# A second set of folded weights in the memory of the second block's first input, and folds split in two halves between other products

## The chip, the cores and the metric

The program runs on one core of a Trainium2 chip. The metric is device time in microseconds (us) of one execution; lower is better. The kernel before took 842.19 us as the median of three runs (839.94 to 844.63).

The engines are named as in the profile: PE is the matrix engine, PEld its weight loads, DVE the vector engine, ACT the scalar engine, POOL the GpSimd engine, SP the queue that issues the transfers. PE writes its products into eight accumulator banks (128 partitions by 512 floats each); ACT and DVE read them from there.

## The reference

The inputs are double-precision for the weights and single-precision in the kernel's arithmetic. What is computed, cut to what matters:

```python
def _attn_ref(q, k, v, phi):                 # 4 samples, 8 heads, 576 rows, head size 64, 32 memory slots
    a = softmax(phi, axis=2)
    k_m, v_m = einsum('bhsm,bhsd->bhmd', a, k), einsum('bhsm,bhsd->bhmd', a, v)
    attn = softmax(q @ k_m.T / sqrt(64))     # 576 x 32 for each sample and head
    return attn @ v_m

x = attention output, heads side by side     # 2304 x 512
y = ((x @ w_a) * (x @ w_b)) @ w_out          # first block, 1536 hidden features
h = y @ w_in                                 # second block, 2048 hidden features
out = (h * sigmoid(1.702 * h)) @ w_out2      # 2304 x 512
```

## The kernel before

**Folded weights.** The attention output is never formed. Since x is attn times v_m, the kernel multiplies the small v_m of a sample into the weights first ("fold") and then the attention into the result ("gated"). A folded weight belongs to one sample and one group of hidden features.

**Tiles and stages.** The first block goes through its 1536 hidden features in 6 groups g of 256 (w_a and w_b side by side, so 512 columns). In each group there are four samples b, each in two halves u of 288 rows. Samples 0 and 1 are called half A of a group here (pb = 0 in the code), samples 2 and 3 half B (pb = 1). Three kinds of products stand on PE, each in sets of 4 products:

- **fold** (line 637, matmuls on line 648): v_m of two samples (tile vhl) times one of the four row blocks r of the weights (tile wab_hl). 4 products, one for each r, of 3 matmuls with 512 columns. Each product fills one bank and has four readers: for each of the two samples ACT copies its half of the partitions to the high part of eff (line 663) and DVE subtracts to get the low part (line 665).
- **gated** (line 671, matmuls on line 687): the folded weights eff times attn. 4 products (j = 0, 1; w_a and w_b) of 6 matmuls with 288 columns. ACT copies the w_a product to gr (line 699), DVE multiplies the w_b product into it (line 702), ACT rounds the result to g1 (line 257), and POOL or DVE subtracts the rest (line 251).
- **proj** (line 708, matmuls on line 719): g1 times w_out. 4 products of 6 matmuls with 288 columns; DVE adds each to acc (line 736).

Every operand is split in a high and a low part, and each product is made in three passes. The folded weights of the samples of a half are in two tiles, eff (even sample) and eff_b (odd sample). Both halves of a group use these two tiles, so a fold can only be written when the gated products of the half before have been read.

**Weights.** Each group has 6 pieces of weights (4 of wab, 2 of w_out). A piece arrives as raw 64-bit words in one of three raw tiles and is decoded to single precision in one of four dm tiles: ACT (line 339), DVE or POOL (line 341), and then DVE three times (lines 345, 349, 354). From dm it is split into wab_hl or whl, by ACT (line 257) and POOL or DVE (line 251). There are four wab_hl tiles, one set; a tile is released by the fold of half B, which is the last to read it.

**What sets the order.** The program is written out in order by a planner (class Order). It keeps an estimated clock for each engine and lets one stream of work after another issue its next operation; a stream with a smaller priority number wins where two could start at about the same time. The planner also chooses the bank for each product (the one that it believes free first) and, where two engines can do a step, the engine. What it writes down is fixed: on the chip each engine runs its instructions in that order and waits for what they need. main() is the stream that gives the order of the products on PE: for each half, both gated sets of the first sample, the proj set left over from the half before (late), a gated set, a proj set, a gated set, then the fold for the half after, then two proj sets.

The tiles yhl[0, HI] and yhl[0, LO] (called y0_0 and y0_1) hold the first half of the second block's input, 4 x 1152 numbers for each partition. They are written only in the last group (split_y), and lie unused until then.

Of the kernel before, what the change touches and what calls it, by code (L numbers as in the profile page):

```python
# [15 lines left out]
HI, LO = 0, 1  # L16
# [130 lines left out]
def tile_mem_attention_moe_moe2(  # L147
# [16 lines left out]
    B, H, S, D = q.shape  # L164
# [13 lines left out]
    NHG = H // HG  # L178
# [4 lines left out]
    CW = G1 * P  # L183
    NG1 = F1 // CW
# [34 lines left out]
    eff_t = [p1.tile([P, NHG, 2, 2 * CW], F32R, name="eff")]  # L219
# [366 lines left out]
    def close_attention():  # L586

        for n in range(NU):
            for e in range(2):
                yield "mark", "attn", n, e  # L590
        for c in range(NHG):
            yield "mark", "eff", 0, B - 1, c, 0
        for s in list(bank_a.free):
            bank_m.free.append(s)
        pa.release()
        od.handicap[DVE] = W1
        nonlocal py, pz
        py = tc.alloc_tile_pool(name="py", bufs=1, side="right", reuse_waits="tile")
        for i in (HI, LO):
            yhl[0, i] = py.tile([P, KD, HT], F32R, name=f"y0_{i}")  # L600
        whl_s.free += slots(py, 1, [P, 2 * KD * G2 * P], "whl_b", F32R).free
        pz = tc.alloc_tile_pool(name="pz", bufs=1, side="right", reuse_waits="tile")
        wab_s.free += slots(pz, 2 * NHG, [P, 2 * 2 * CW], "wab_hl", F32R).free
        eff_t.append(pz.tile([P, NHG, 2, 2 * CW], F32R, name="eff_b"))
        vhl.extend(pz.tile([P, 2, 2 * NHG, P], F32R, name=f"vhl{i}") for i in range(B // 2))
        od.spawn(8, split_memory())


    py, pz, vhl, yhl, g1_t = None, None, [], {}, {}

    def fold0(b):
        for c in range(NHG):
# [21 lines left out]
                t1 = yield from hi_lo(t, dst[:, HI], dst[:, LO], src, 2 * D)  # L634
                od.mark(t1, "vhl", b, e)

    def fold(g, pb):
        t0 = 0.0
        for b in (2 * pb, 2 * pb + 1):
            for e in range(2):  # L640
                t0 = max(t0, (yield "mark", "vhl", b, e))
        outs = []
        for r in range(2 * NHG):
            t = max(t0, (yield "mark", "wab", g, r, 0))
            t, ps = yield PE, t, 650, bank_m
            w = w_ab_view(wt["wab", g, r][0])
# [11 lines left out]
                )  # L658

    def fold_out(t, g, b, c, part, half, ps, left):  # L660
        hi, lo = (eff_t[b % 2 if g else 0][half, c, i, :] for i in (HI, LO))
        t, _ = yield ACT, t, act(512, True)
        nc.scalar.activation(out=hi, in_=ps[0][half, :], func=AF.Copy)  # L663
        t, _ = yield DVE, t, dve(512)
        nc.vector.tensor_tensor(out=lo, in0=ps[0][half, :], in1=f32(hi), op=ALU.subtract)  # L665
        left[0] -= 1
        if left[0] == 0:
            bank_m.release(ps, t)
        od.mark(t, "eff", g, b, c, part)

    def gated(g, b, u):
        t0 = 0.0
        for c in range(NHG):
            t0 = max(t0, (yield "mark", "attn", b * NHG + c, u))
            for i in range(2 if g else 1):
                t0 = max(t0, (yield "mark", "eff", g, b, c, i))
        e = eff_t[b % 2 if g else 0]
        g1 = yield "slot", g1_s
        g1_t[g, b, u] = g1
        for j in range(G1):  # L680
# [167 lines left out]
    def main():  # L848
# [11 lines left out]
        for g in range(1, NG1):  # L860
            for pb in range(B // 2):
                b = 2 * pb
                yield from gated(g, b, 0)
                yield from gated(g, b, 1)
                if late is not None:
                    yield from proj(*late)
                yield from gated(g, b + 1, 0)
                yield from proj(g, b, 0)
                yield from gated(g, b + 1, 1)
                if pb + 1 < B // 2:  # L870
                    yield from fold(g, pb + 1)
                elif g + 1 < NG1:
                    yield from fold(g + 1, 0)
                else:
                    break
                yield from proj(g, b, 1)
                yield from proj(g, b + 1, 0)
                late = g, b + 1, 1
# [86 lines left out]
```

## Time and profile before

| | us |
|---|---|
| median of 3 runs | 842.19 |
| the profiled execution | 843.73 |
| its span, first to last instruction | 841.9 |
| PE busy in the span | 814.8 (97%) |
| DVE busy | 565.5 (67%) |
| ACT busy | 366.5 (44%) |
| POOL busy | 336.9 (40%) |

The profile shows one execution. A timeline gives for each run of like instructions the start from the span's start, the length, the engine, the line and the operands, and in square brackets how long the engine sat idle before it and what ended that. A window gives busy time of each engine in a stretch, and the clock that PE was granted there as a share of its full one. The first block's groups 1 to 5 lie between 137 and 426 us; before them are attention and group 0, behind them the second block. In the second block, 416 us long, the idle times before PE's instructions in the timeline come to 1.8 us.

### The profile page before, as it was taken

How to read it: one execution, taken by the hardware profiler on the slowest of the kernel's cores; microseconds unless marked ns; L12 is line 12 of the kernel's file. 1: busy time of each engine (PE TensorE's matmuls, PEld its weight loads, DVE VectorE, ACT ScalarE, POOL GpSimd, SP SyncE). 2: the span in 40 equal slices, each digit the busy share in tenths (PEclk: the TensorE clock that was granted, in tenths of full speed). 3: DMA queues.
4: the chain of work that ended last, by engine and by line, in shares of the span. 5: the costliest groups of instructions: out<-in, count | busy, mean ns of one | idle time of the engine just before them, and what ended most of it. 6: DMA issues, size and time to landing. Idle time of an engine off the chain costs nothing.

```text
span 841.9 us, 13723 instructions
## 1 busy us (share of the span) xinstructions
PE 814.8 (97%) x5280; PEld 745.3 (89%) x5280; DVE 565.5 (67%) x1004; ACT 366.5 (44%) x794; POOL 336.9 (40%) x310
## 2 busy tenths in 40 slices
PE   8999999999989999989999999999999999999996
PEld 7766799989989989989997999898989899999995
DVE  3997779995894984987589573846647475443333
ACT  3676776643643643545564332423333242322220
POOL 1432145662642733725675441614334252332220
PEclk9998999999999999999999999999999999999999
DMA  9687102140040130131013030111103000000134
GB/s 339 230 262 231 55 1 100 52 150 2 26 125 1 51 101 1 54 97 50 2 51 100 1 100 1 51 51 47 54 0 99 2 26 1 2 0 1 26 88 113
DMA packets 33025, 57.77 MB, mean 69 GB/s; under 512 B 3520, under 2 KB 15808, under 8 KB 32960
## 3 DMA queue, kind: packets, MB, share of 16 engines
q1 hardware_dynamic: 32384, 55.85, 21.5%
q10 hardware_dynamic: 576, 1.05, 0.4%
q8 instruction: 41, 0.67, 0.3%
q14 instruction: 24, 0.20, 0.1%
HBM read 52.17 MB, written 4.72 MB: 68 GB/s over the span
## 4 chain that ended last, share of the span: by engine, by line
PE 68%; DVE 19%; issue 4%; ACT 3%; DMA 2%; POOL 2%; SPq 0%; DVEq 0%; ACTq 0%; POOLq 0%
PE bank L816 22%; PE bank L775 22%; PE bank L687 10%; PE bank L719 9%; DVE eff L665 3%; DVE acc L736 3%; DVE dm L349 2%; DVE dm L354 2%; DVE dm L345 2%; DVE eff_b L665 2%; DVE gr L702 2%; DMA kv<-in_v_dram 1%; DVE g L251 1%; PE bank L529 1%; PE bank L489 1%
## 5 line engine op out<-in xcount | busy, mean ns | idle before, releaser
L816 PE MATMUL bank<-wo,g 128*128 128x512 f32 x864 | 206.3, 392 | 1.4 <-ACT g L257 1.1
L251 POOL TENSOR_TENSOR g<-sg,g 128x384 fp32r<-128x384 f32 x95 | 101.8, 1074 | 227.6 <-ACT g L257 189.8
L816 PEld LDWEIGHTS bank<-wo,g 128*128 128x128 f32 x864 | 161.4, 188 | 34.3 <-ACT g L257 1.4
L788 DVE TENSOR_TENSOR sg<-bank,sg 128x384 f32<-128x384 f32 x96 | 53.3, 556 | 114.7 <-ACT sg L786 114.7
L786 ACT ACTIVATE sg<-bank 128x384 f32<-128x384 f32 x96 | 47.0, 490 | 178.7 <-PE bank L775 178.2
L832 DVE TENSOR_TENSOR acc<-bank,acc 128x512 f32<-128x512 f32 x126 | 86.9, 689 | 52.8 <-PE bank L816 52.4
L251 POOL TENSOR_TENSOR g<-gr,g 128x288 fp32r<-128x288 f32 x76 | 68.7, 905 | 133.8 <-ACT g L257 133.6
L775 PE MATMUL bank<-y,whl_a 128*128 128x384 f32 x576 | 104.8, 337 | 0.4 <-DVE sg L788 0.4
L775 PE MATMUL bank<-y,whl_b 128*128 128x384 f32 x576 | 104.1, 336 | 0.0
L775 PEld LDWEIGHTS bank<-y,whl_a 128*128 128x128 f32 x576 | 101.2, 188 | 2.6 <-DVE sg L788 0.8
L775 PEld LDWEIGHTS bank<-y,whl_b 128*128 128x128 f32 x576 | 100.9, 188 | 1.9
L687 PE MATMUL bank<-attn,eff 128*128 128x288 f32 x672 | 94.7, 298 | 1.0 <-ACT eff L663 0.7
L687 PEld LDWEIGHTS bank<-attn,eff 128*128 128x128 f32 x672 | 90.8, 189 | 2.9 <-issue 1.4
L719 PE MATMUL bank<-g,whl_a 128*128 128x288 f32 x576 | 85.4, 302 | 4.8 <-DVE acc L736 2.4
L719 PEld LDWEIGHTS bank<-g,whl_a 128*128 128x128 f32 x576 | 79.8, 192 | 9.6 <-DVE acc L736 3.3
L719 PE MATMUL bank<-g,whl_b 128*128 128x288 f32 x576 | 82.3, 299 | 4.9 <-DVE acc L736 2.5
L719 PEld LDWEIGHTS bank<-g,whl_b 128*128 128x128 f32 x576 | 79.1, 191 | 7.1 <-DVE acc L736 3.7
L257 ACT ACTIVATE g<-gr 128x288 fp32r<-128x288 f32 x96 | 42.7, 444 | 81.6 <-DVE gr L702 81.6
L257 ACT ACTIVATE g<-sg 128x384 fp32r<-128x384 f32 x96 | 50.4, 525 | 62.4 <-DVE sg L788 62.0
L736 DVE TENSOR_TENSOR acc<-bank,acc 128x288 f32<-128x288 f32 x160 | 67.3, 449 | 13.2 <-PE bank L719 12.5
L341 POOL TENSOR_SCALAR dm<-dm 128x512 f32<-128x512 f32 x35 | 59.4, 1697 | 30.5 <-ACT dm L339 30.5
L702 DVE TENSOR_TENSOR gr<-bank,gr 128x288 f32<-128x288 f32 x96 | 43.3, 451 | 40.6 <-PE bank L687 37.9
(108 smaller groups left out, 1032.8 us busy)
## 6 DMA issues: line engine op xcount, KB each, us to landing
raw<-in_moe_w_out_dram SPq DMA_DIRECT2D x28, 512.0 KB, 3.6
raw<-in_moe_w_in_dram SPq DMA_DIRECT2D x16, 512.0 KB, 3.8
raw<-in_moe_w_a_dram SPq DMA_DIRECT2D x21, 256.0 KB, 2.9
raw<-in_moe_w_b_dram SPq DMA_DIRECT2D x21, 256.0 KB, 3.3
q<-in_q_dram SPq DMA_DIRECT2D x8, 576.0 KB, 6.2
out_dram<-acc SPq DMA_DIRECT2D x72, 64.0 KB, 1.7
kv<-in_k_dram SPq DMA_DIRECT2D x8, 320.0 KB, 4.4
kv<-in_v_dram SPq DMA_DIRECT2D x8, 320.0 KB, 5.2
```

The costliest lines, as they stand in the source:

```text
L251: (nc.gpsimd if e == POOL else nc.vector).tensor_tensor(out=dst, in0=in0, in1=in1, op=op)
L257: nc.scalar.activation(out=hi, in_=src, func=AF.Copy)
L341: (nc.vector if e == DVE else nc.gpsimd).tensor_scalar(out=mf, in0=mf, scalar1=2.0 ** -15, scalar2=None, op0=ALU.max)
L687: nc.tensor.matmul(ps[0][:, :U], e[:, c, sw, i * CW + j * P:i * CW + (j + 1) * P], attn(b, mv, c, u * U, U), start=(n == 0), stop=(n == 3 ...
L702: nc.vector.tensor_tensor(out=gr[0], in0=pb[0][:, :U], in1=gr[0], op=ALU.mult)
L719: nc.tensor.matmul(ps[0][:, :U], w[:, sw, j, mb * P:(mb + 1) * P], g1[0][:, j, mv, :], start=(n == 0), stop=(n == 3 * G1 - 1),)
L736: nc.vector.tensor_tensor(out=dst, in0=ps[0][:, :U], in1=dst, op=ALU.add)
L775: nc.tensor.matmul(ps[0][:, :N2], w[:, sw, c, j * P:(j + 1) * P], yhl[half, mv][:, c, o:o + N2], start=(n == 0), stop=(n == 3 * KD - 1),)
L786: nc.scalar.activation(out=sg[0], in_=ps[0][:, :N2], func=AF.Sigmoid, scale=1.702)
L788: nc.vector.tensor_tensor(out=sg[0], in0=ps[0][:, :N2], in1=sg[0], op=ALU.mult)
L816: nc.tensor.matmul(ps[0], g2[0][:, j, sw, s * P:(s + 1) * P], w[:, mv, j, :], start=(n == 0), stop=(n == 3 * G2 - 1),)
L832: nc.vector.tensor_tensor(out=dst, in0=ps[0], in1=dst, op=ALU.add)
```

## The change

The second half of the samples gets folded weights of its own. In groups 1 to 4 the folds for half B are written into the memory of y0_0 and y0_1 (2048 of their 4608 numbers for each partition), which the second block needs only later. In group 5, where that memory is about to be filled, half B uses eff and eff_b as before.

Since the fold for the half after then no longer writes over what the present half reads, it is moved forward and cut in two: the products of row blocks 0 and 1 stand between the first sample's two gated sets, those of row blocks 2 and 3 behind the second sample's first gated set. This holds for 8 folds, those of half B in groups 1 to 4 and of half A in groups 2 to 5. The first fold, that for half A of group 1, and the one for half B of group 5 stay where they were. The number of products is the same.

```diff
         eff_t.append(pz.tile([P, NHG, 2, 2 * CW], F32R, name="eff_b"))
+        for i in (HI, LO):
+            flat = yhl[0, i].rearrange("p k t -> p (k t)")[:, :NHG * 2 * 2 * CW]
+            eff_t.append(flat.rearrange("p (c i f) -> p c i f", c=NHG, i=2))
...
+    def eff_of(g, b):
+
+        if g == 0:
+            return eff_t[0]
+        return eff_t[b % 2 + (2 if b // 2 == 1 and g < NG1 - 1 else 0)]
...
-    def fold(g, pb):
+    def fold(g, pb, pairs=range(2 * NHG)):
...
-        for r in range(2 * NHG):
+        for r in pairs:
...
-        hi, lo = (eff_t[b % 2 if g else 0][half, c, i, :] for i in (HI, LO))
+        hi, lo = (eff_of(g, b)[half, c, i, :] for i in (HI, LO))
...
-        e = eff_t[b % 2 if g else 0]
+        e = eff_of(g, b)
...
                 b = 2 * pb
+                nxt = (g, pb + 1) if pb + 1 < B // 2 else (g + 1, 0)
+
+                early = nxt[0] < NG1 and eff_of(g, b) is not eff_of(nxt[0], 2 * nxt[1])
                 yield from gated(g, b, 0)
+                if early:
+                    yield from fold(*nxt, range(NHG))
                 yield from gated(g, b, 1)
                 if late is not None:
                     yield from proj(*late)
                 yield from gated(g, b + 1, 0)
+                if early:
+                    yield from fold(*nxt, range(NHG, 2 * NHG))
                 yield from proj(g, b, 0)
                 yield from gated(g, b + 1, 1)
-                if pb + 1 < B // 2:
-                    yield from fold(g, pb + 1)
-                elif g + 1 < NG1:
-                    yield from fold(g + 1, 0)
-                else:
+                if nxt[0] == NG1:
                     break
+                if not early:
+                    yield from fold(*nxt)
                 yield from proj(g, b, 1)
                 yield from proj(g, b + 1, 0)
                 late = g, b + 1, 1
```

The planner's order changes with it. On PE this is the end of half B of group 2 before: the fold for group 3, then two proj sets (tiles: bank = accumulator bank, wab_hl and vhl = operands of the fold, g1 and whl = operands of proj, y0 and eff = folded weights).

```order
L648 MATMUL bank0_83<-wab_hl0_1412,vhl0_1417 128x512 x3
L648 MATMUL bank2_85<-wab_hl1_1413,vhl0_1417 128x512 x3
L648 MATMUL bank6_89<-wab_hl2_1414,vhl0_1417 128x512 x3
L648 MATMUL bank5_88<-wab_hl3_1415,vhl0_1417 128x512 x3
L719 MATMUL bank1_84<-g1_0_105,whl_a0_99 128x288 x6
L719 MATMUL bank3_86<-g1_0_105,whl_a0_99 128x288 x6
L719 MATMUL bank4_87<-g1_0_105,whl_a0_99 128x288 x6
L719 MATMUL bank7_90<-g1_0_105,whl_a0_99 128x288 x6
L719 MATMUL bank0_83<-g1_1_106,whl_a0_99 128x288 x6
L719 MATMUL bank1_84<-g1_1_106,whl_a0_99 128x288 x6
L719 MATMUL bank3_86<-g1_1_106,whl_a0_99 128x288 x6
L719 MATMUL bank4_87<-g1_1_106,whl_a0_99 128x288 x6
```

In the changed kernel the last 12 products of the same half are these:

```order
L695 MATMUL bank3_86<-attn1_82,y0_1_1407 128x288 x6
L695 MATMUL bank1_84<-attn1_82,y0_1_1407 128x288 x6
L695 MATMUL bank6_89<-attn1_82,y0_1_1407 128x288 x6
L695 MATMUL bank2_85<-attn1_82,y0_1_1407 128x288 x6
L727 MATMUL bank4_87<-g1_0_105,whl_a0_99 128x288 x6
L727 MATMUL bank5_88<-g1_0_105,whl_a0_99 128x288 x6
L727 MATMUL bank7_90<-g1_0_105,whl_a0_99 128x288 x6
L727 MATMUL bank3_86<-g1_0_105,whl_a0_99 128x288 x6
L727 MATMUL bank0_83<-g1_1_106,whl_a0_99 128x288 x6
L727 MATMUL bank1_84<-g1_1_106,whl_a0_99 128x288 x6
L727 MATMUL bank6_89<-g1_1_106,whl_a0_99 128x288 x6
L727 MATMUL bank2_85<-g1_1_106,whl_a0_99 128x288 x6
```

The fold has gone from there (its second half now stands one proj set further ahead), a gated set is in its place, and the banks of the two proj sets are written again 7 products or more after their last use, where before bank1, bank3 and bank4 were written again after 5.

On DVE this is the work around the fold at the same end of half B before (dm and raw = a weight piece being decoded, gr = a gated product, acc = a proj):

```order
L354 SCALAR_TENSOR_TENSOR dm2_97<-raw1_92,dm2_97 128x512
L345 TENSOR_SCALAR dm3_98<-dm3_98 128x512
L349 SCALAR_TENSOR_TENSOR dm3_98<-raw2_93,dm3_98 128x512
L702 TENSOR_TENSOR gr1_109<-bank3_86,gr1_109 128x288
L354 SCALAR_TENSOR_TENSOR dm3_98<-raw2_93,dm3_98 128x512
L702 TENSOR_TENSOR gr2_110<-bank7_90,gr2_110 128x288
L665 TENSOR_TENSOR eff_104<-bank0_83,eff_104 64x512
L665 TENSOR_TENSOR eff_104<-bank2_85,eff_104 64x512
L665 TENSOR_TENSOR eff_b_1416<-bank0_83,eff_b_1416 64x512
L665 TENSOR_TENSOR eff_104<-bank6_89,eff_104 64x512
L665 TENSOR_TENSOR eff_104<-bank5_88,eff_104 64x512
L736 TENSOR_TENSOR acc_80<-bank1_84,acc_80 128x288
```

In the changed kernel the first half of that fold comes earlier in half B, and its subtractions stand so on DVE:

```order
L710 TENSOR_TENSOR gr2_110<-bank2_85,gr2_110 128x288
L345 TENSOR_SCALAR dm0_95<-dm0_95 128x512
L349 SCALAR_TENSOR_TENSOR dm0_95<-raw2_93,dm0_95 128x512
L710 TENSOR_TENSOR gr0_108<-bank4_87,gr0_108 128x288
L354 SCALAR_TENSOR_TENSOR dm0_95<-raw2_93,dm0_95 128x512
L673 TENSOR_TENSOR eff_104<-bank1_84,eff_104 64x512
L673 TENSOR_TENSOR eff_104<-bank5_88,eff_104 64x512
L673 TENSOR_TENSOR eff_b_1416<-bank1_84,eff_b_1416 64x512
L710 TENSOR_TENSOR gr1_109<-bank6_89,gr1_109 128x288
L673 TENSOR_TENSOR eff_b_1416<-bank5_88,eff_b_1416 64x512
L710 TENSOR_TENSOR gr2_110<-bank2_85,gr2_110 128x288
L744 TENSOR_TENSOR acc_80<-bank3_86,acc_80 128x288
```

Before, five of the fold's eight subtractions stood in a row directly behind the last decode of the group and ahead of the acc of proj. Now four of them stand in the middle of half B, with the gated products' operations between them, again directly behind the decode, and the other four come further on.

The planner also shares some work out anew: DVE takes over 6 subtractions for wab_hl and whl and 3 operations of line 341 from POOL and gives it 6 subtractions for g1, so that DVE has 3 operations more than before and POOL 3 fewer. ACT and SP have as many as before, and SP's order is the same. Everything from the second block's start stands in the same order on PE.

## Rows read from the trace of the kernel before

**Rows 1.** Timeline of PE: start, length, line, operands, count, [idle before, releaser].
```profile
193.60 6.53 PE L687 MATMUL bank<-attn,eff 128*128 128x288 f32 x48
199.96 3.34 PE L719 MATMUL bank<-g,whl_b 128*128 128x288 f32 x24
203.14 3.36 PE L687 MATMUL bank<-attn,eff_b 128*128 128x288 f32 x24
...
235.04 3.49 PE L719 MATMUL bank<-g,whl_a 128*128 128x288 f32 x24 [0.32 <-DVE acc L736]
238.37 3.36 PE L687 MATMUL bank<-attn,eff_b 128*128 128x288 f32 x24
241.57 2.89 PE L648 MATMUL bank<-wab_hl,vhl 128*128 128x512 f32 x12
244.30 3.33 PE L719 MATMUL bank<-g,whl_a 128*128 128x288 f32 x24
248.58 1.06 PE L719 MATMUL bank<-g,whl_a 128*128 128x288 f32 x6 [0.95 <-DVE eff_b L665]
250.50 2.68 PE L719 MATMUL bank<-g,whl_a 128*128 128x288 f32 x18 [0.87 <-DVE acc L736]
253.03 6.52 PE L687 MATMUL bank<-attn,eff 128*128 128x288 f32 x48
```

**Rows 2.** Windows: stretch, length, busy (count) of PE PEld DVE ACT POOL, clock, DMA.
```profile
137.40:193.60 56.20, 53.69 (x380) 51.79 (x381) 52.63 (x93) 32.32 (x69) 32.77 (x26) 1.00 0.30 94
193.60:253.03 59.43, 57.29 (x411) 55.63 (x410) 46.42 (x87) 28.70 (x60) 27.63 (x24) 1.00 0.18 54
253.03:313.91 60.88, 58.53 (x410) 56.88 (x409) 47.50 (x90) 28.63 (x60) 27.46 (x24) 0.97 0.18 53
313.91:375.19 61.28, 58.84 (x410) 57.02 (x409) 47.07 (x87) 28.71 (x60) 27.22 (x24) 0.97 0.17 53
```

**Rows 3.** Chain of waits in time, 300 to 320: start, length, what.
```profile
303.97 0.68 DVE dm L354
304.65 0.38 DVE gr L702
...
305.50 0.49 ACT eff L663
...
306.01 0.68 DVE eff L665
...
309.52 0.47 DVE acc L736
...
310.03 4.04 PE bank L719 x18
```

**Rows 4.** Windows, columns as above: a calm stretch, and one with a stall.
```profile
193.60:221.80 28.20, 28.20 (x207) 27.72 (x205) 16.41 (x35) 13.57 (x29) 8.81 (x10) 1.00 0.00 1
...
307.00:313.90 6.90, 4.93 (x24) 4.70 (x25) 6.67 (x14) 3.28 (x6) 0.00 (x0) 0.75 0.15 55
```

**Rows 5.** Timeline of DVE and POOL, 282 to 312.
```profile
282.36 2.06 DVE L341 TENSOR_SCALAR dm<-dm 128x512 f32<-128x512 f32 x2
...
288.44 1.62 POOL L251 TENSOR_TENSOR whl_a<-dm,whl_a 128x512 fp32r<-128x512 f32 x1
...
289.20 1.41 DVE L354 SCALAR_TENSOR_TENSOR dm<-raw,dm 128x512 uint32<-128x512 uint32 x1
...
296.04 0.41 DVE L345 TENSOR_SCALAR dm<-dm 128x512 uint32<-128x512 uint32 x1
...
297.45 0.69 DVE L354 SCALAR_TENSOR_TENSOR dm<-raw,dm 128x512 uint32<-128x512 uint32 x1
...
309.52 1.55 DVE L736 TENSOR_TENSOR acc<-bank,acc 128x288 f32<-128x288 f32 x4
```

**Rows 6.** Timeline of DVE in the first group.
```profile
140.28 1.25 DVE L341 TENSOR_SCALAR dm<-dm 128x512 f32<-128x512 f32 x1 [0.19 <-ACT dm L339]
...
153.18 0.46 DVE L702 TENSOR_TENSOR gr<-bank,gr 128x288 f32<-128x288 f32 x1 [0.81 <-ACT gr L699]
```

More of the change, by code (lines that the diff above doesn't have):

```diff
@@ L641, in fold @@
                 t0 = max(t0, (yield "mark", "vhl", b, e))
-        outs = []
-        for r in range(2 * NHG):
+        for r in pairs:
             t = max(t0, (yield "mark", "wab", g, r, 0))
```

## The prediction

> **What bounds the kernel now.** The times come first: PE is busy for 814.8 of 841.9 us, so PE sets the time, and only its waits and its clock can be won back, since the number of products does not change. I read the timeline of PE next, because it shows where it waits [rows 1]. For the price of work without waits it gives: two gated sets from 193.60 to 199.96, so 3.18 us a set; one on eff_b from 238.37 to 241.57, 3.20; a proj set from 199.96 to 203.14, 3.18; a fold from 241.57 to 244.30, 2.73. A group has 8 gated sets, 8 proj sets and 2 folds: 4 x 3.18 + 4 x 3.20 + 8 x 3.18 + 2 x 2.73 = 56.4 us. Group 1 has one proj set fewer, and its window starts 0.5 us into a gated set, so 52.7.
>
> The windows by group [rows 2] show 56.20, 59.43, 60.88 and 61.28 us. The losses are 3.5, 3.0, 4.5 and 4.9, together 15.9 us. The reader should see in rows 1 where they lie in group 2: 0.32 idle at 235.04, and above all behind the fold. The four proj products at 244.30 are followed at 248.58 and not at 247.48 (1.10 lost, released by DVE eff_b), the next 6 matmuls take until 250.50 where 0.80 would do (1.12 lost, released by DVE acc). The other groups have the same two waits at the end of half B.
>
> Why is the bank late there? The chain of waits [rows 3] tells it for group 3: DVE finishes a weight decode (L354, 303.97 to 304.65), only then the gr of a gated product, then ACT can round that g until 305.50, and only behind that ACT copies the fold (L663) and DVE subtracts it (306.01). The fold was long done on PE by then; its four banks, with 16 reads, are still held when proj wants them again, and the acc of proj stands behind five subtractions, until 309.52. So DVE lags by some 4 us at that point, and PE pays. In groups 3 and 4 it pays twice: the clock of the stretch with the stall was 0.75 of full [rows 4], so it ran partly at 1.2 GHz in place of 2.4, after the two waits; 18 proj matmuls took 4.04 us [rows 3] against 2.53 in group 2 [rows 1], 1.5 us more.
>
> **The change part by part.** PE: 8 folds are moved, none added, cost 0. What they leave behind is the two waits at the end of half B: there are no fold banks in that place now, and the proj banks come back after 7 products or more and not after 5. With no decode behind half B's first part either, DVE has time there. I take these losses and the clock's 1.5 us in groups 3 and 4 as gone: -15.9 us.
>
> DVE: the lag does not vanish, it moves. The fold for half B releases the wab tiles, and so sets when the next 6 pieces are split and decoded. It stood at the end of half A, so the decode filled half B and half A was calm (DVE 16.41 of 28.20 us [rows 4]). Now it stands early in half A, in two parts, and the decode fills the rest of half A beside the second part. I walk through a middle group with t = 0 at the first part of the fold in half A on PE. Without waits the second part is at 10.9 to 12.3, the first part of the fold in half B at 28.2 to 29.6, the gated set behind it ends at 32.8, and a proj set comes from there. DVE begins the dense stretch at about 5.8 and has to go through 49 operations up to the first subtraction of the fold in half B (the order rows of DVE show the end of them): 16 acc and 6 gr, at 0.39 (four in 1.55 [rows 5]) 8.6 us; 4 subtractions of the fold at 0.68 [rows 3] 2.7; 12 of lines 349 and 354, between 0.69 alone and 1.41 [rows 5], 0.80 taken, 9.6; 6 of line 345, at 0.41 [rows 5] or more, 0.5 taken, 3.0; 3 of line 341 at 1.03 (two in 2.06 [rows 5]), 3.1; and 2 weight subtractions, which no row has on DVE, by the same bounds 0.69 to 1.41, 0.9 taken, 1.8. That is 28.8, so DVE comes to this fold at 34.6, 5 us after its end on PE. The 0.80 is the value with which these prices add up, to within 0.3, to the 22.7 us that DVE needed for the old dense stretch from 282.36 to 305.0 [rows 3, 5].
>
> What is late next: at 34.4 PE wants the bank of a gated product whose copy to gr stands on ACT behind two copies of the fold, and these behind a gr of DVE at about 33.2. That copy ends at 35.3 to 35.4, so PE waits 1.0 us. It is one wait in each of groups 2, 3 and 4, 3.0 us. Bounds: with all 12 decode steps at 0.69 DVE is 1.3 earlier and the wait is 0; with all at 1.41 it is 7.3 later and the wait is up to 8.3.
>
> Here a rule speaks against the change. The rows show a decode step on DVE of 1.41 us from 289.20 on, while POOL had a subtraction from 288.44 to 290.06, and one of 0.69 at 297.45 [rows 5]. The Trainium skill (SBUF — State Buffer, Who interferes with whom) says that DVE and GpSimd share one pair of ports, held as an exclusive lock for a whole instruction, for DVE instructions with two inputs in SBUF among others; the trace agrees, since the 1.41 step ends 0.55 us behind the end of POOL's. By that rule alone, with a POOL instruction beside each step, the sum would be that of the third rival below; by the mix that the trace shows it is the 1.0 us.
>
> Group 1 is the worst place: DVE had no idle time worth the name from 140.28 to 152.4 (it sat idle 0.81 us before 153.18 [rows 6]), since the first decode falls there, and it is busy for 52.63 of 56.20 us [rows 2]. Eight subtractions of a fold at 0.68 come into that stretch, 5.4 us that so far began after 153. PE can run ahead of DVE by some products, since there are eight banks; between 0 (all absorbed) and 5.0 (nothing) I take the middle, 2.5, and it falls on the proj and gated sets behind the second half of the fold, near 154.
>
> Edits taken at nothing: the tiles y0_0 and y0_1 are first written in group 1 after the attention's last step, and again by the second block's input only in group 5, a whole half after their last reader; if either had to wait, ACT would be held at its copy of the fold and PE behind it. The weights of a first half-fold are there about 21 us before it (split at 7, wanted at 28), those of the second about 20; that cover would have to shrink to 0 first. SP's order is unchanged; the loads go out when a raw tile is free, and the DMA share is 0.16 to 0.30 in these windows [rows 2], so they have room. Group 5 and the second block keep their order on PE, with 1.8 us idle before and after.
>
> The sum: -15.9 + 2.5 + 3.0 = -10.4 us. The profiled execution took 843.7 (span 841.9 and 1.8 around it), so 833.3 for one like it. It was 1.5 above the median of 842.19, so I forecast 831.8.
>
> **The rivals.** A measurement of this kernel can tell about 0.5%, 4.2 us, from no change.
>
> *No wait is left.* For it: over a whole group DVE is busy for 46 to 48 us of the 56.4 that PE needs [rows 2], and the second part of half B is now free of decode. Against it: the dense stretch above. All 15.9 us gone gives 826.3.
>
> *The waits come back in half A.* DVE runs 3 us later than in my walk (1.05 us for each of the 12 steps), and PE waits 4 us in each of groups 2 to 4 and 3 in group 1, which is 15 of the 15.9: 841. For it: fold and decode now stand together where they were apart. Against it: the 0.80 fits the old dense stretch.
>
> *Slower.* The same place, but the lock beside every step: 1.41 for all 12, a wait of 8.3 in each of three groups, 5.0 in group 1, and the clock down after each of the four, 1.5 each [rows 1, 3]: 24.9 + 5.0 + 6.0 = 35.9 against 15.9, so 862. It decides from 1.09 us a step on: then three groups wait 4.5 each, and with group 1's 2.5 nothing is won. The trace bears out single steps of 1.41, not all. The rule of the Trainium skill above (SBUF — State Buffer, Who interferes with whom) is this rival's.
>
> *It doesn't do what it says.* The early halves wait for weights or for the tiles, and the stall only moves in front of the fold. The order has them in place and the covers are 20 us: hardly. 842.
>
> **How the numbers follow.** My forecast 0.60, no wait left 0.15, waits back 0.15, slower 0.06, not as said 0.04. The range goes from 826.0, which takes in the case without waits, to 839.0, which takes in the light end of the second rival; about 0.2 lies outside. Faster by over 0.5% is forecast, first rival and 0.04 of the second: 0.79; within 0.5% the rest of it and the last: 0.15; slower 0.06.
>
> **What would show it.** Right: no wait of a proj behind a fold at the end of half B; groups of 57 to 58 us and group 1 of 55; clock 1.00 in all; the one new wait before the proj set behind half B's first half-fold, released by ACT's gr or DVE's fold. Wrong: a group over 59 us, decode steps of over 1.0 us on the mean in half A, or a clock below 0.98 in any group's window.

## The result, and the profile after

The changed kernel took 833.97 us as the median of four runs (832.59 to 834.85), the kernel before 843.41 beside it (839.94 to 847.38). The ratio is 0.9893, with a 95% interval of 0.9858 to 0.9928: 1.1% faster. The forecast was 831.8, with a range of 826.0 to 839.0. The profiled execution took 834.6 us, with a span of 832.4; before it was 841.9, so 9.5 us are to be explained.

The page of the changed kernel: the line on PE, the chain by engine, and the two proj groups.

```profile
PE 811.4 (97%) x5280; PEld 743.9 (89%) x5280; DVE 562.1 (68%) x1007; ACT 363.4 (44%) x794; POOL 330.7 (40%) x307
...
PE 83%; DVE 8%; issue 3%; ACT 2%; POOL 1%; DMA 1%; DVEq 0%; SPq 0%; ACTq 0%; POOLq 0%
...
L727 PE MATMUL bank<-g,whl_a 128*128 128x288 f32 x576 | 82.6, 297 | 0.2 <-POOL whl_a L251 0.2
...
L727 PE MATMUL bank<-g,whl_b 128*128 128x288 f32 x576 | 80.7, 297 | 0.6 <-ACT gr L707 0.6
```

PE still sets the time. What is new is that its proj products hardly wait: 0.2 and 0.6 us of idle time in the whole span.

The windows of groups 1 to 5, which answer to rows 2 (columns as there):

```profile
137.06:195.93 58.87, 55.64 (x381) 53.48 (x382) 54.32 (x96) 31.40 (x69) 33.12 (x26) 0.97 0.29 90
195.93:252.49 56.56, 56.56 (x411) 55.53 (x409) 45.66 (x87) 28.07 (x60) 25.27 (x23) 1.00 0.18 57
252.49:308.95 56.46, 56.46 (x411) 55.46 (x410) 45.65 (x87) 27.94 (x60) 24.89 (x23) 1.00 0.18 57
308.95:365.51 56.56, 56.56 (x411) 55.53 (x409) 45.59 (x87) 27.95 (x60) 25.30 (x23) 1.00 0.20 57
365.51:416.49 50.98, 50.94 (x375) 50.09 (x373) 31.10 (x63) 27.57 (x64) 29.99 (x34) 1.00 0.07 22
```

In groups 2 to 4 PE is busy from end to end, at the full clock (1.00): 56.5 us against 59.43, 60.88 and 61.28 [rows 2], and 56.4 was the price of the work alone. Group 1 went the other way, from 56.20 to 58.87 us, although its work is worth 52.7. So the gains are 2.9, 4.4 and 4.7 us in groups 2 to 4, group 1 costs 2.7 of them, and the remaining 0.2 is the difference of the stretches before and behind.

The end of half B in group 2, where rows 1 had waits of 0.95 and 0.87 us, in the timeline of PE:

```profile
238.35 1.54 PE L656 MATMUL bank<-wab_hl,vhl 128*128 128x512 f32 x6
239.74 3.33 PE L727 MATMUL bank<-g,whl_a 128*128 128x288 f32 x24
242.91 3.36 PE L695 MATMUL bank<-attn,y 128*128 128x288 f32 x24
246.10 6.54 PE L727 MATMUL bank<-g,whl_a 128*128 128x288 f32 x48
```

The two proj sets at the end run as one piece of 48 matmuls. And group 1, from its second half-fold on:

```profile
152.80 2.14 PE L695 MATMUL bank<-attn,eff_b 128*128 128x288 f32 x12
156.96 2.68 PE L695 MATMUL bank<-attn,eff_b 128*128 128x288 f32 x12 [2.02 <-DVE acc L744]
159.43 7.23 PE L727 MATMUL bank<-g,whl_b 128*128 128x288 f32 x48
...
174.26 1.75 PE L727 MATMUL bank<-g,whl_b 128*128 128x288 f32 x12
176.61 1.87 PE L727 MATMUL bank<-g,whl_b 128*128 128x288 f32 x12 [0.60 <-ACT gr L707]
```

The start times tell what is lost. Twelve gated matmuls take 1.60 us without a wait, so the ones from 152.80 were through at 154.40, and the next started 2.56 later. These took until 159.43, 2.47 in place of 1.60, and the 48 proj matmuls until 166.50, 7.07 in place of 6.36: 1.6 us at a lower clock, as the windows of the two stretches show.

```profile
157.00:160.00 3.00, 3.00 (x15) 3.00 (x16) 2.94 (x6) 1.42 (x4) 2.36 (x2) 0.62 0.01 3
160.00:166.50 6.50, 6.50 (x48) 6.50 (x48) 6.50 (x13) 2.91 (x6) 4.38 (x4) 0.91 0.36 106
```

A mean of 0.62 says that most of that stretch ran at 1.2 GHz, the lower of the two levels, half of the full 2.4. What DVE did while PE waited:

```profile
150.99 2.10 DVE L341 TENSOR_SCALAR dm<-dm 128x512 f32<-128x512 f32 x2
...
154.41 0.68 DVE L349 SCALAR_TENSOR_TENSOR dm<-raw,dm 128x512 uint32<-128x512 uint32 x1
155.01 1.40 DVE L673 TENSOR_TENSOR y<-bank,y 64x512 fp32r<-64x512 f32 x2
156.44 1.19 DVE L744 TENSOR_TENSOR acc<-bank,acc 128x288 f32<-128x288 f32 x3
```

The tile is named y because the new folded weights lie in its memory. DVE stood in the decode and in the subtractions of the moved fold, and the acc that gives the bank back came behind both.

### The profile page after: what moved, and what is told of

It reads as the page before. It is cut to its first block, busy times and chain, and to the rows that moved or that the text cites. A ratio compares the mean times of both kernels' runs of the same rounds, so it can differ in the third digit from the quotient of the medians.

```text
span 832.4 us, 13727 instructions
## 1 busy us (share of the span) xinstructions
PE 811.4 (97%) x5280; PEld 743.9 (89%) x5280; DVE 562.1 (68%) x1007; ACT 363.4 (44%) x794; POOL 330.7 (40%) x307
## 4 chain that ended last, share of the span: by engine, by line
PE 83%; DVE 8%; issue 3%; ACT 2%; POOL 1%; DMA 1%; DVEq 0%; SPq 0%; ACTq 0%; POOLq 0%
PE bank L824 23%; PE bank L783 23%; PE bank L727 15%; PE bank L695 14%; PE bank L656 2%; DVE dm L345 1%; DVE dm L354 1%; DVE dm L349 1%; PE bank L489 1%; PE bank L628 1%; PE bank L529 1%; DVE gr L710 1%; PE bank L404 1%; DMA phi<-in_phi_dram 1%; DMA raw<-in_moe_w_b_dram 1%
## 5 line engine op out<-in xcount | busy, mean ns | idle before, releaser
L251 POOL TENSOR_TENSOR g<-gr,g 128x288 fp32r<-128x288 f32 x82 | 75.6, 924 | 122.5 <-ACT g L257 122.0
L727 PE MATMUL bank<-g,whl_a 128*128 128x288 f32 x576 | 82.6, 297 | 0.2 <-POOL whl_a L251 0.2
L727 PEld LDWEIGHTS bank<-g,whl_a 128*128 128x128 f32 x576 | 78.1, 188 | 3.6 <-issue 1.3
L695 PE MATMUL bank<-attn,eff 128*128 128x288 f32 x480 | 68.5, 297 | 1.0 <-ACT eff L671 0.7
L341 POOL TENSOR_SCALAR dm<-dm 128x512 f32<-128x512 f32 x32 | 55.3, 1728 | 34.6 <-ACT dm L339 34.6
L695 PEld LDWEIGHTS bank<-attn,eff 128*128 128x128 f32 x480 | 64.9, 188 | 3.2 <-issue 1.4
```

Of the source, the lines that this page charges most:

```text
L251: (nc.gpsimd if e == POOL else nc.vector).tensor_tensor(out=dst, in0=in0, in1=in1, op=op)
L341: (nc.vector if e == DVE else nc.gpsimd).tensor_scalar(out=mf, in0=mf, scalar1=2.0 ** -15, scalar2=None, op0=ALU.max)
L695: nc.tensor.matmul(ps[0][:, :U], e[:, c, sw, i * CW + j * P:i * CW + (j + 1) * P], attn(b, mv, c, u * U, U), start=(n == 0), stop=(n == 3 ...
L727: nc.tensor.matmul(ps[0][:, :U], w[:, sw, j, mb * P:(mb + 1) * P], g1[0][:, j, mv, :], start=(n == 0), stop=(n == 3 * G1 - 1),)
```

## The experiments

Each kernel was run beside the kernel before, whose medians were 842.99, 844.21 and 842.97 us in the three series. Theory lag is the prediction's: PE loses time where DVE comes late out of a dense stretch of decode and the banks are still held.

**The second set alone.** The folds stay where they were, whole.

```diff
-                early = nxt[0] < NG1 and eff_of(g, b) is not eff_of(nxt[0], 2 * nxt[1])
+                early = False
```

> The second set of folded weights is kept, the folds stand whole at the end of each half as in the kernel before. Theory lag (the waits at the end of half B come from DVE being late with the weight decode, which holds up ACT's copies of the fold and so the banks): no gain, within 3 us of the kernel before, and the waits of 2 to 3 us behind each fold at the end of half B stay. Rival shared tiles (the fold has to wait until the last gated set has read eff and eff_b): most of the gain is here already, 8 to 10 us faster than before.

Measured: 843.08 us, ratio 1.001 (0.9986 to 1.0034). A group of its profile, and the waits at the end of it:

```profile
193.79:255.07 61.28, 58.92 (x410) 57.02 (x409) 47.05 (x87) 28.63 (x60) 27.38 (x24) 0.97 0.17 52
```

```profile
249.21 1.06 PE L727 MATMUL bank<-g,whl_a 128*128 128x288 f32 x6 [1.21 <-DVE eff_b L673]
251.14 4.09 PE L727 MATMUL bank<-g,whl_a 128*128 128x288 f32 x18 [0.87 <-DVE acc L744]
```

The waits of rows 1 are all there, and the time is that of the kernel before, as theory lag expected. The memory is worth nothing by itself; the gain comes with the order that it allows.

**Banks strictly in turn.** In the kernel before, proj at the end of half B takes a bank again after five products. Here the planner may give out in groups 1 to 5 only the bank that was used longest ago.

```diff
+    def ready(self):
+        return [s for s in self.free if s is self.used[0]] if self.ring else self.free
...
+        bank_m.ring = True
         late = None
         for g in range(1, NG1):
```

> The kernel before, with the banks of the first block given out strictly in turn in groups 1 to 5, so that each is written again after exactly 8 products and none after 5; folds late and whole. Rival banks (proj waits because its banks come back after 5 products): the waits at the end of half B go, 12 to 16 us faster than before. Theory lag: the second wait of 0.9 us turns into a wait for a bank of the fold, which DVE empties late all the same; 0 to 5 us faster than before, and 2 us or more of waits a group stay.

Measured: 859.34 us, ratio 1.0197 (1.0173 to 1.0222): 16 us slower, where both theories had no loss or a gain, so the size was missed by both. At the end of half B in group 1 of its profile:

```profile
189.09 1.06 PE L725 MATMUL bank<-g,whl_b 128*128 128x288 f32 x6 [1.14 <-DVE eff_b L671]
192.70 4.69 PE L725 MATMUL bank<-g,whl_b 128*128 128x288 f32 x18 [2.55 <-DVE eff_b L671]
```

Both waits are now for subtractions of the fold (eff_b), the second one 2.55 us in place of 0.87. In turn, proj has to take the fold's four banks, which DVE holds longest, and may not pass them by for a bank of proj that is free sooner. So the early reuse was not the fault; by these rows it was the planner's way round the late banks.

**Less decode in the kernel before.** Everything stands in the same order, but one of DVE's decode steps is left out for the weights of groups 2 to 5.

```diff
-        nc.vector.scalar_tensor_tensor(
-            out=mu, in0=hw, scalar=0xC0000000, in1=mu, op0=ALU.bitwise_and, op1=ALU.bitwise_or
-        )
+        if not (name[0] in ("wab", "o1") and name[1] >= 2):
+            nc.vector.scalar_tensor_tensor(
+                out=mu, in0=hw, scalar=0xC0000000, in1=mu, op0=ALU.bitwise_and, op1=ALU.bitwise_or
+            )
```

> The kernel before, without the second of the three DVE decode steps of each weight piece (the step of line 349) for groups 2 to 5 of the first block; its output is not the reference's. The planner still counts the step, so everything else stands in the same order. DVE has 6 steps of 0.8 to 0.9 us fewer in each group, about 5 us, which is the lag. Theory lag: the waits behind the fold at the end of half B and the lower clock in groups 3 and 4 go, 12 to 16 us faster than before. Rivals shared tiles and banks: the waits stay, less than 4 us faster.

Measured: 830.58 us, ratio 0.9859 (0.9835 to 0.9883). It is 12.4 us faster than the kernel before beside it, at the light end of the 12 to 16 that theory lag expected. Groups 2 and 4 of its profile:

```profile
188.01:245.20 57.19, 56.74 (x410) 55.56 (x409) 42.10 (x81) 28.64 (x60) 25.83 (x24) 1.00 0.18 56
...
302.36:360.92 58.56, 57.00 (x411) 55.57 (x410) 45.08 (x85) 28.63 (x60) 26.77 (x24) 1.00 0.19 55
```

Group 2 lost 3.0 us before and loses 0.8 here, with six DVE instructions fewer (81 against 87). Group 4, whose decode is in part that of the second block's weights and keeps its step, still loses 2.2 of its 4.9. The folds stand where they stood, so it was DVE's lateness that cost the time, as theory lag has it.

**Group 1's fold of half B whole and late, all else as changed.**

```diff
-                early = nxt[0] < NG1 and eff_of(g, b) is not eff_of(nxt[0], 2 * nxt[1])
+                early = (g, pb) != (1, 0) and nxt[0] < NG1 and eff_of(g, b) is not eff_of(nxt[0], 2 * nxt[1])
```

> The changed kernel, with the fold for half B of group 1 whole and at the end of half A, as in the kernel before; the other 7 folds early and in two parts. Theory: group 1 lost 6.2 us in the changed kernel because the first early fold brings eight subtractions into a stretch in which DVE has no time left; without it group 1 loses 1 to 3.5 us, so 3 to 5 us faster than the changed kernel, 829 to 831. Rival: group 1 is bound by its decode wherever the fold stands; 834, as the changed kernel.

Measured: 830.76 us (828.09 to 832.38), ratio 0.9859 (0.9824 to 0.9894). Its group 1, and the one wait of over 0.5 us in it:

```profile
136.90:191.83 54.93, 53.49 (x380) 51.90 (x381) 50.95 (x93) 32.05 (x69) 33.63 (x27) 1.00 0.26 80
```

```profile
183.77 1.87 PE L695 MATMUL bank<-attn,y 128*128 128x288 f32 x12 [1.34 <-DVE acc L744]
```

Group 1 goes from 58.87 to 54.93 us, at the full clock. The loss of 6.2 falls to 2.2 when eight subtractions leave the stretch in which DVE decodes without a pause.

**Each fold whole at the first early place.**

```diff
                 if early:
-                    yield from fold(*nxt, range(NHG))
+                    yield from fold(*nxt)
...
-                if early:
-                    yield from fold(*nxt, range(NHG, 2 * NHG))
```

> The changed kernel, but each fold stands whole, with its four products, at the first of its two early places. Theory lag: the eight subtractions of a fold come at once, four banks are held together, and in half B they meet DVE at the end of its dense stretch, where the changed kernel had only about 0.25 us to spare. PE then has two banks fewer there and wants one some 1.6 us sooner, so it waits 1.0 to 2.5 us in each of groups 2 to 4, and group 1 loses 0 to 2 more than its 6.2 us: 837 to 843. Rival, the cut in two is worth nothing and only the early place counts: 833 to 835, no wait in groups 2 to 4.

Measured: 846.88 us (845.12 to 849.65), ratio 1.0044 (1.0027 to 1.0061). It is slower than the kernel before, and beyond what either theory expected. Group 2 of its profile, the waits in the middle of half B, and ACT and DVE at the fold there:

```profile
196.72:256.54 59.82, 57.84 (x410) 55.52 (x409) 47.59 (x87) 28.12 (x60) 24.80 (x23) 1.00 0.17 54
```

```profile
236.68 1.06 PE L727 MATMUL bank<-g,whl_a 128*128 128x288 f32 x6 [1.26 <-DVE eff_b L673]
238.09 2.65 PE L727 MATMUL bank<-g,whl_a 128*128 128x288 f32 x18 [0.35 <-ACT gr L707]
```

```profile
234.59 1.41 DVE L673 TENSOR_TENSOR eff<-bank,eff 64x512 fp32r<-64x512 f32 x2 [0.99 <-ACT eff L671]
```

```profile
232.66 0.45 ACT L257 ACTIVATE g<-gr 128x288 fp32r<-128x288 f32 x1 [3.44 <-DVE gr L710]
```

The fold began on PE at 228.98, and DVE came to it at 234.59, 5.6 us later; before that, ACT had waited for a late gr of DVE. But in these rows DVE waits for ACT too, and a whole fold needs eight copies and eight subtractions until its four banks are free. So it stayed open here whether DVE's lag or the draining of four banks at a time cost the 3.3 us of each group. The run "whole and early, with less decode" below tells them apart.

**Less decode in the changed kernel.** The edit of the run with less decode above, made on the changed kernel.

> The changed kernel without the decode step of line 349 for the pieces of w_a, w_b and the first output weights of groups 2 to 5; the sign bits are left out of these weights, and the order of everything else stays as it was. Theory lag: group 1 loses 6.2 us because DVE has the decode and eight subtractions of a fold in one stretch; with about nine steps of 0.7 to 0.8 us taken from group 1 its waits of 2.02, 0.60 and 0.41 us and the 1.6 us at the lower clock go: group 1 from 58.9 to 53 to 55 us, groups 2 to 4 as they are at 56.5, so 828 to 830.5. Rival, group 1 waits because of its place (tiles of the second set, copies on ACT, banks), not because DVE is late: group 1 stays above 57 us and the time at 833 to 834.5.

Measured: 830.15 us (829.65 to 830.68). Its group 1:

```profile
134.83:190.29 55.46, 53.63 (x380) 51.95 (x381) 49.66 (x87) 31.33 (x69) 31.69 (x26) 1.00 0.30 96
```

With nine DVE instructions fewer (87 against 96) group 1 loses 2.8 us and not 6.2, at the full clock, and the wait of 2.02 is one of 1.21. Groups 2 to 4 stay at 56.5. The fold's place is the same as in the changed kernel, so place alone is not the cause. It did not fall quite as far as expected (53 to 55).

**More decode in the changed kernel.** The same step twice, for the pieces of groups 3 to 5.

```diff
-        nc.vector.scalar_tensor_tensor(
-            out=mu, in0=hw, scalar=0xC0000000, in1=mu, op0=ALU.bitwise_and, op1=ALU.bitwise_or
-        )
+        for _ in range(2 if name[0] in ("wab", "o1") and name[1] >= 3 else 1):
+            nc.vector.scalar_tensor_tensor(
+                out=mu, in0=hw, scalar=0xC0000000, in1=mu, op0=ALU.bitwise_and, op1=ALU.bitwise_or
+            )
```

> The changed kernel with the decode step of line 349 done twice for the pieces of groups 3 to 5, which gives the same weights: six steps of about 0.78 us more on DVE in the dense stretch of half A of the groups concerned, 4.7 us. Theory lag, with the spare time of about 0.25 us that the trace of the changed kernel shows at the fold of half B: PE waits about 4.4 us in groups 2 and 3, 2 to 4.4 in group 4 and 0 to 2 in group 1, 11 to 15 us in all, and up to 1.5 more in each of these groups if the clock falls: 845 to 853. Rival, DVE has room in groups 2 to 4, since it is busy for only 45.6 of 56.5 us there: 834 to 837.

Measured: 847.75 us (846.42 to 848.79), 13.8 over the changed kernel. Groups 1, 2 and 4:

```profile
136.30:198.34 62.04, 57.45 (x380) 55.08 (x381) 57.38 (x100) 31.52 (x69) 33.09 (x26) 0.94 0.27 86
198.34:259.42 61.08, 58.06 (x410) 55.71 (x409) 50.11 (x93) 27.99 (x60) 24.45 (x23) 1.00 0.17 53
...
320.54:378.89 58.35, 57.34 (x410) 55.69 (x409) 47.50 (x89) 27.93 (x60) 25.36 (x23) 1.00 0.18 55
```

So theory lag holds, in its size too: groups 2 and 3 lost 4.5 and 4.7 us more, group 4 1.8, and group 1 3.2, with the clock at 0.94 (up to 2 was expected there, and up to 1.5 more if the clock fell). In group 2, six more DVE steps (93 against 87) made DVE busy for 4.45 us more and the group 4.52 longer; in group 4, two more (89 against 87) made it 1.91 and 1.79. The dense stretch gives the work back one for one, though DVE is idle for 11 of the 56.5 us of a group: its idle time lies before and behind that stretch, where it is of no use.

**In group 1, the other fold one place later too.** On top of the late fold of half B, the first part of the fold for group 2 stands where its second part was, and the second where the old fold was.

```diff
-                early = nxt[0] < NG1 and eff_of(g, b) is not eff_of(nxt[0], 2 * nxt[1])
+                early = g > 1 and nxt[0] < NG1 and eff_of(g, b) is not eff_of(nxt[0], 2 * nxt[1])
...
+                if (g, pb) == (1, 1):
+                    yield from fold(*nxt, range(NHG))
                 yield from proj(g, b, 0)
...
-                    yield from fold(*nxt)
+                    yield from fold(*nxt, range(NHG if (g, pb) == (1, 1) else 0, 2 * NHG))
```

> The changed kernel, but in group 1 the fold of half B stands whole and late, as in the run with only that, and the fold of half A of group 2 stands one place later: its first part where the second was, its second part where the old fold was. Theory lag: the one wait that was left in group 1 there, 1.34 us released by an acc of DVE at 183.77, goes or shrinks, since DVE has then done more of its decode: group 1 at 53.5 to 55 us, 828 to 830.5. Rival: the old late place brings back its own waits behind the fold (1.25 and 0.87 us in group 1 with the second set alone): group 1 at 56 to 57, 831 to 833.

Measured: 832.41 us (831.6 to 833.11), ratio 0.9869 (0.9833 to 0.9905). The rival was right: group 1 took 56.90 us, with these waits,

```profile
183.35 1.87 PE L695 MATMUL bank<-attn,y 128*128 128x288 f32 x12 [1.67 <-DVE acc L744]
...
192.67 1.85 PE L727 MATMUL bank<-g,whl_b 128*128 128x288 f32 x12 [1.33 <-DVE acc L744]
```

the second of them behind the old late place. Only the first of the two moves pays.

**Whole and early, with less decode.** The whole fold at the first early place, and the decode step left out as above.

> The kernel with each fold whole and early, but without the decode step of line 349 for the pieces of w_a, w_b and the first output weights of groups 2 to 5; the sign bits are left out of these weights, and the order of everything else stays as it was. With the step, groups 2 to 4 took 59.8 us each, 3.3 over the changed kernel. Theory lag: ACT stood idle for 3.44 us before the copies of half B's fold, for a gr of DVE that was late; with six steps less (about 4.5 us) DVE is there in time, and groups 2 to 4 fall to 56.5 to 57.2: 828 to 833. Theory drain: a whole fold holds four banks until ACT has made eight copies of 0.6 us and DVE eight subtractions of 0.68, 5.5 us, with the copies of the gated set behind them on ACT, and this is so however early DVE is there: groups 2 to 4 stay at 58.3 to 59.8, and the time at 836 to 844.

Measured: 832.82 us (832.01 to 834.34). Groups 2 and 4, and DVE at the fold of half B in group 2, which began on PE at 223.10:

```profile
191.63:248.21 56.58, 56.58 (x411) 55.60 (x409) 42.01 (x81) 28.34 (x60) 24.30 (x23) 1.00 0.19 57
...
304.72:363.19 58.47, 57.10 (x410) 55.65 (x409) 45.13 (x85) 28.35 (x60) 24.80 (x23) 1.00 0.19 55
```

```profile
226.13 1.41 DVE L674 TENSOR_TENSOR eff<-bank,eff 64x512 fp32r<-64x512 f32 x2 [0.99 <-ACT eff L672]
```

DVE is at the fold 3.0 us after its start and not 5.6, and the loss of groups 2 and 3 is gone (56.58 and 56.51 us), with the fold as whole as it was. In group 4, where only two steps are missing, 1.9 us stay. So draining four banks does not cost the time by itself, and the lag does. With two banks, the changed kernel bears 4.1 us (below) without a wait; with four, 3.0 is borne and 5.6 costs 3.3. Those lags differ, so they do not tell whether the number of banks counts. Rows of like lag, of half B's fold in group 4, speak for it: the first two are of the run with more decode (two banks), the others of this run (four).

```profile
352.53 1.54 PE L657 MATMUL bank<-wab_hl,vhl 128*128 128x512 f32 x6
358.04 1.40 DVE L674 TENSOR_TENSOR eff<-bank,eff 64x512 fp32r<-64x512 f32 x2
...
336.19 2.90 PE L657 MATMUL bank<-wab_hl,vhl 128*128 128x512 f32 x12
341.21 1.41 DVE L674 TENSOR_TENSOR eff<-bank,eff 64x512 fp32r<-64x512 f32 x2 [0.99 <-ACT eff L672]
```

With two banks DVE came 5.5 us behind PE's start, and the gated set and the proj set behind that half-fold took 1.3 us longer than their price (353.90 to 361.56, in place of 6.38); with four it came 5.0 behind, and they took 1.9 longer (338.93 to 347.23). So the number of banks seems to count too, but the orders of the two kernels differ in more than that, and no run changes it alone. The cut in two, with the later place of its second part, also brings DVE to the fold of group 2 earlier (4.1 us against 5.6); in all it is worth 12.9 us between the medians of the whole fold and of the changed kernel, and how that divides stays open.

**The changed kernel, and the one with group 1's fold late, side by side.** No new edit.

> The changed kernel as it is, beside the next run on the same chip. 833 to 835, group 1 at 58.9 us.

> The changed kernel with the fold of half B of group 1 whole and late, once more, beside the changed kernel on the same chip. If the 3.2 us between them are the waits and the lower clock of group 1, they are there again: 829.5 to 832, 2.5 to 4 us below the changed kernel, group 1 at 55 us. If they were chance, both are at 833.

Measured: 833.48 us (833.17 to 834.06) for the changed kernel, 831.68 (830.68 to 832.49) for the other. The group windows, of the first and of the second:

```profile
136.60:195.43 58.83, 55.67 (x381) 53.51 (x381) 54.32 (x96) 31.47 (x69) 33.11 (x26) 0.97 0.30 90
```

```profile
136.01:190.84 54.83, 53.45 (x380) 51.90 (x381) 50.85 (x93) 31.84 (x69) 33.61 (x27) 1.00 0.26 81
```

The difference of the medians is 1.8 us here, less than the 2.5 expected, and 3.2 between the earlier ones; the eight runs of the one (828.09 to 832.49) all lie below the eight of the other (832.59 to 834.85). The version with group 1's fold late beats both kernels, by 0.2 to 0.4% over the changed one. Its group 1 is 4.0 us shorter in these two profiles, but 1.5 of that is lost again behind it, by a lower clock in the second block (0.66 from 446 to 451), which the earlier profile of the same kernel does not have (the last section shows it).

## Why the prediction was right, and where its sizes were off

**The losses that go.** Right. All waits at the end of half B went, and the lower clock of groups 3 and 4 with them. That the lag of DVE behind the decode was their cause is shown by the run with less decode on the kernel before, that the order and not the memory takes them away by the run with the set alone.

**The wait at half B's first half-fold, groups 2 to 4.** The step was right, its size was not: 1.0 us each was forecast, and 0.1 to 0.2 is lost in the whole group. In the timeline of DVE in group 2 (on PE the first half-fold of half A began at 199.09, that of half B at 227.37):

```profile
204.73 0.75 DVE L251 TENSOR_TENSOR wab_hl<-dm,wab_hl 128x512 fp32r<-128x512 f32 x1 [0.33 <-ACT wab_hl L257]
...
231.51 1.40 DVE L673 TENSOR_TENSOR eff<-bank,eff 64x512 fp32r<-64x512 f32 x2
```

And the copy on ACT:

```profile
232.84 0.41 ACT L707 ACTIVATE gr<-bank 128x288 f32<-128x288 f32 x1
```

The dense stretch had the forecast 49 operations, but took 26.8 us and not 28.8. From start to next start, the twelve steps of lines 349 and 354 took 9.6, on the mean 0.80 as chosen. The two terms that were too dear are line 341 (0.69 each and not 1.03, 1.0 us of the 2.0) and line 345 (0.39 and not 0.5, 0.65); acc and gr give 0.3 more. For line 341 the forecast had one row of two with 2.06 us [rows 5]. DVE came to the fold 32.4 us after the first part in half A, not 34.6, and ACT's copy of gr was through at 233.25, with PE wanting that bank at about 233.5 by the forecast's walk. The time to spare is a quarter of a microsecond or so, and the run with more decode agrees: 4.5 us of work for 4.5 us of time.

**Group 1.** The place was right (PE stalls near 154), the term too small: 6.2 us against 2.5, and above its bound of 5.0. Two things failed in that step. The middle between 0 and 5.0 was taken, though rows 2 and 6 had DVE busy for 52.63 of 56.20 us there; without the clock's share the loss still came to 4.6, near the upper end. And the bound left the clock out: 1.6 us at the lower level, which I had put into the rival "slower" alone. The two runs that took the fold or the decode step out of that stretch brought the loss to 2.2 and 2.8. So it is the two together on DVE that cost there; what makes up the rest was not taken apart. One of the prediction's own signs of being wrong was met here: the clock of group 1's window is 0.97, below the 0.98 that it named, and with 58.87 us the group stays just under the 59 of another.

**The sum.** Forecast -15.9 + 2.5 + 3.0 = -10.4; measured -15.9 + 6.2 + 0.4 = -9.3 in groups 1 to 4, and -9.5 between the spans. The two terms were off by +3.7 and -2.6 us, so most of the error cancelled, and the sum was nearer than either of them: that much was luck. Of the 2.2 us between 831.8 and 833.97 they leave 1.1; most of the rest is the start, since the median of the kernel before was 843.41 beside the changed one and not 842.19. The forecast pattern, groups of 57 to 58 us with one new wait each and group 1 at 55, was not what came.

**The rivals.** "No wait is left" is true of groups 2 to 4 and false of group 1. "The waits come back in half A" and "slower" did not happen, but the run with more decode shows that they were near: 4.5 us more of DVE's work in each of groups 2 and 3 take away what was won there. For "slower" the prediction took 1.5 us for a fall of the clock, from 4.04 us against 2.53; but the first is a length and the second runs to the next start. From start to next start the 18 matmuls took 3.88 us (310.03 to 313.91 [rows 2, 3]), so 1.35 more. The sum does not use this number. Of the lock: in that stretch one decode step on DVE beside POOL took 1.60 us to the next start (L354 at 210.86, with subtractions of POOL from 210.61 on), steps alone 0.60. The rule of the Trainium skill (SBUF — State Buffer, Who interferes with whom) agrees with the single steps; the sum followed their mix. "It doesn't do what it says" fell: the half-folds waited for no weights, and SP's order and the second block, 415.9 us against 415.7, are as they were.

## What to carry to other kernels

When PE waits for a bank, ask what the engine that empties it does before that, and try another place for the product, or a cut, so that this engine is less far behind when the banks are wanted: here the memory alone was worth nothing, and the early place without the cut was slower than the kernel before. An engine that is busy for 80% of a stage can, as here, have no slack in a dense stretch of it; doubling one step there shows at once whether it has. Where the same step repeats over groups, look at the first group apart, since its work falls together with what is only there.

## What the runs showed of the hardware that was not expected

PE's clock answered to single waits in a way that the prediction had not foreseen. After one wait of 2.02 us in group 1 the clock was 0.62 from 157 to 160, and in the second profile of the same kernel, after one of 2.00, 0.52:

```profile
157.00:160.00 3.00, 3.00 (x15) 3.00 (x14) 2.94 (x6) 0.97 (x3) 2.81 (x2) 0.52 0.01 3
```

Single waits of 1.34 and 1.67 us left it at 1.00 in their groups, as did the pair 1.26 and 0.35 of the whole early folds. The pair 0.95 and 0.87 left it at 1.00 in group 2 of the kernel before [rows 1, 2], and so did 1.25 and 0.87 in its group 1 (at 189.18 and 191.11). But behind 1.21 and 0.87 with the second set alone, the 18 proj matmuls took 3.93 us to the next start (251.14 to 255.07) in place of 2.53. And the same waits in the same kernel can end either way. With group 1's fold late, PE waits 1.07 us for ACT and then 0.35 for POOL early in the second block, in both profiles; these are the 13 matmuls behind, in the first profile and in the second:

```profile
447.59 3.25 PE L824 MATMUL bank<-wo,g 128*128 128x512 f32 x13 [0.36 <-POOL g L251]
...
446.59 4.84 PE L824 MATMUL bank<-wo,g 128*128 128x512 f32 x13 [0.35 <-POOL g L251]
```

So the lengths of such waits alone do not tell whether the clock falls, and what does, these runs do not show. What a fall costs they do: 1.6 us in group 1 in both profiles of the changed kernel, after waits of 2.0, 1.4 behind the pair with the second set alone, and 1.6 here. Much of the spread between runs of one kernel goes with it: of the sixteen runs of the kernel before in the second series, the shortest took 840.3 us at a mean clock of 0.996, the longest 846.36 at 0.988.
